# Fused attention and two feed-forward layers: adjacent heads as pairs, keys on 128 partitions, whole w_in transfers, TensorE turning the first q

## The chip, the cores and the metric

One core of one Trainium2 chip runs the kernel. The metric is the device time of one execution in microseconds. The kernel before was timed three times. Besides that there is a profiled execution, from which all rows below come.

## The reference

```python
# q, k, v: (8 batches, 8 heads, 576 tokens, 64); float32. w_in etc.: float64
k_p = k.reshape(B, H, 72, 8, D).mean(axis=3)          # keys and values pooled by 8
v_p = v.reshape(B, H, 72, 8, D).mean(axis=3)
scores = scale * np.matmul(q, k_p.transpose(0, 1, 3, 2))
attn = softmax(scores)                                 # exp(x - max) / (sum + 1e-9)
x = matmul(attn, v_p) -> (4608 tokens, 512)            # heads side by side
h = x @ w_in; g = h * np.cos(h); y = g @ w_out         # 512 -> 2048 -> 512
g = y @ w_gate; silu = g / (1 + exp(-g))               # 512 -> 1536
out = (silu * (y @ w_val)) @ w_out2                    # 1536 -> 512
```

The weights come as float64 and are converted on the chip, two 32-bit words to one number.

## The kernel before

The stages run on one another. Attention goes batch by batch (8 batches of 576 tokens) in tiles of 128 tokens, the fifth of 64 (`TILES`). The first feed-forward layer goes in 9 blocks of 512 tokens, each of 16 slots (one slot a block of 128 of the 2048 hidden rows): `pe_h` makes a hidden block, the scalar and vector engines its cosine, `pe_y` adds its part of the output, two slots later. The attention of batches 1 to 7 is spread over those slots by the tables MID, LATE, EXP and NORM with START. Batch 0 runs alone ahead of slot 0 by the string `program`: s is the scores of a tile (`do_s`, and then `do_qt` of the next tile), x its softmax, p the turning of the probabilities, a the product with the values, V and K and U the pooling sums, f a few steps of weight conversion, i and o loads of w_in and w_out, q the load of batch 1's q, X the split of the first block of x. The second layer follows from slot 128 on in products of a fast matrix scheme; the change doesn't touch it.

Heads are paired for TensorE: two heads of 64 dimensions lie on the 128 partitions. Before, head p and head p + 4 make pair p (`(r p)` in the views). `kT` holds a pair's keys in blocks, so that one matmul gives both heads' scores.

q: `load_q` (line 143) reads a batch in four transfers, one for each half r of the heads and each half e of the 64 dimensions, into 32 partitions each, in runs of 32 numbers (128 bytes); ACT_QUEUE says which batches' halves the scalar engine (ACT) issues instead of SyncE (SP). `do_qt` (line 257) turns a tile in blocks of 32x32 on VectorE (DVE).

Keys: the raw keys lie on 72 partitions, one for each pooled position, 8 tokens x 64 numbers in a row. `pool_sum` halves the row three times by additions (lines 190 and 192). Batch 0's raw keys come in two transfers into `kst`, batch 1's in four into buffers of w_in (`load_kv1`), both are summed on DVE. Later batches come in pieces by `do_raw`, one piece a slot, and are summed on GpSimd (POOL). `prep_k` turns the sums on TensorE and ACT scales them into `kT`.

Weights: `cv_load` (line 438) issues a unit's load. A unit of w_in is 128 rows of 512 numbers (4 KB a row), read as two halves of 64 rows to 64 partitions, because a pair's two heads stand 256 rows apart in w_in. A unit of w_out is 128 rows in one transfer. The conversion is a run of DVE instructions (lines 445, 456, 462, 467, 473) with one on ACT (451).

Order: the code is traced in Python, and the Tile layer's scheduler puts each engine's instructions in an order from its own estimate of times. On an engine that order is fixed. A transfer's issue waits on its queue for what it needs, and so does all behind it.

Of the kernel before, what the change touches and what calls it, by code (L numbers as in the profile page):

```python
# [8 lines left out]
F32 = mybir.dt.float32  # L9
# [16 lines left out]
def fused_kernel(  # L26
# [42 lines left out]
    ACT_QUEUE = {(0, 0), (3, 1), (1, 1), (3, 0), (1, 0)}  # L69
# [14 lines left out]
    xhl = const.tile([P, 2, KC, TB], F32R, name="xhl")  # L84
# [71 lines left out]
    pairs = "(r p) (s l) d -> r s p (l d)"  # L156
    kview = [k[b].rearrange(pairs, r=2, l=POOL) for b in range(B)]
    vview = [v[b, :, : SM * POOL].rearrange(pairs, r=2, l=POOL) for b in range(B)]
    vleft = [v[b, :, SM * POOL :].rearrange("h (s l) d -> h s (l d)", l=POOL) for b in range(B)]

    def load_kv(b, kind, i):

        rows = SP if kind == "k" else P
        t = kvraw[b, kind, i] = p1a.tile([P, POOL * D], F32, name=f"{kind}raw_{b}_{i}", tag="kv", bufs=2)[:rows]
        if kind == "k":
            nc.sync.dma_start(t, kview[b][i % 2, :, i // 2])
# [4 lines left out]
    def load_kv1():  # L171

        for p in range(NP):
            t = wts.tile([P, 2, TB], F32, name=f"k1_{p}", tag=f"wa3{p}")
            nc.sync.dma_start(t[:SP], kview[1][:, :, p].rearrange("r s x -> s r x"))
            kraw1.append(t[:SP])
# [20 lines left out]
    def new_kp(b):  # L197
        kps[b] = p1a.tile([SP, NP, 2, D], F32, name=f"kp_{b}", tag="kp")
# [4 lines left out]
    def sum_kv(b, kind, i):  # L203
        if i == 0:
            (new_kp if kind == "k" else new_vp)(b)
        dst = kps[b][:, i // 2, i % 2] if kind == "k" else vps[b][:, i]
        pool_sum(nc.gpsimd, dst, kvraw.pop((b, kind, i)))

    def prep_k(b):

        kp = kps.pop(b)
        ps = psum.tile([P, NP, SP], F32, name=f"kps_{b}", tag="att", bufs=2)
        for p in range(NP):
            nc.tensor.transpose(ps[:, p], kp[:, p].rearrange("s r d -> s (r d)"), ident[:SP, :SP])
        nc.scalar.mul(kT[0:64, :, 0:SP], ps[0:64], -EXP_SCALE)
        nc.scalar.mul(kT[64:128, :, SP:], ps[64:128], -EXP_SCALE)

    def prep_v(b):
        vmh, vml, vl1, vl2 = (av_tile(nm, b) for nm in ("vmh", "vml", "vl1", "vl2"))
        vp = vps.pop(b)  # L220
        if b < ACTB:
            for r in range(2):
# [5 lines left out]
                mask[:SM].rearrange("q (r p o) -> q r p o", r=2, o=1).to_broadcast([SM, 2, NP, D]),  # L228
# [13 lines left out]
        t = t.rearrange("q (r p) d -> q r p d", r=2)  # L242
# [48 lines left out]
    def do_norm(b, t, pm=None):  # L291
# [16 lines left out]
        for g in range(2):  # L308
            left = pm[:n, H * SM + g * SM : H * SM + (g + 1) * SM].rearrange("q (r p s) -> q p r s", r=2, p=NP)
            if g == 0:  # L310
                nc.vector.tensor_mul(
                    left,
                    e[:, :, SM:].rearrange("q (p r) s -> q p r s", r=2),
                    sm.rearrange("q (p r) o -> q p r o", r=2).to_broadcast([n, NP, 2, SL]),
                )
# [51 lines left out]
    raws = [(b, kind, i) for b in range(2, B) for kind, m in (("k", H), ("v", NP + 1)) for i in range(m)]  # L367

    def do_raw(b, i):
        at = (b - 2) * (H + NP + 1) + i  # L370
# [46 lines left out]
    for b in range(1, B):  # L417
# [3 lines left out]
        if b + 1 < B:  # L421
            for i in range(H + NP + 1):
# [9 lines left out]
    def cv_load(key, src, home=None):  # L432
        st = raw_tile(f"st_{key}") if home is None else wts.tile([P, 2, TB], F32, name=f"st_{key}", tag=home)
        st = st.rearrange("p a t -> p (a t)")
        src = src if isinstance(src, list) else [src]
        m = P // len(src)
        for i, x in enumerate(src):
            nc.sync.dma_start(st[i * m : (i + 1) * m].bitcast(U64), x)
# [46 lines left out]

    def x_split(half):
# [771 lines left out]
```

## Time and profile before

| | us |
|---|---|
| median of 3 timed runs | 1805.19 |
| lowest and highest | 1802.82, 1806.52 |
| the profiled execution | 1804.83 |
| its span | 1803.1 |
| busy: PE, DVE, ACT, POOL | 1737.5, 1263.8, 1066.6, 171.7 |

The span is the time from the core's first instruction to its last. Busy time is the time in which an engine has at least one instruction under way. PE is TensorE's matmuls, PEld its weight loads; SPq and ACTq are transfers' issues on those engines, whose data moves later. The 16 DMA engines are shared by all queues; q1 is SP's, q10 ACT's.

### The profile page before, as it was taken

The page shows a single profiled execution, that of the slowest core. Times are in us where ns is not written, and L with a number is a line of the kernel's source. Part 1 is how long each engine was busy: PE and PEld are TensorE (multiplying, and loading weights), DVE is VectorE, ACT ScalarE, POOL GpSimd, SP SyncE. Part 2 cuts the span into 40 slices and gives each one's busy share as a digit, 9 for nine tenths or more (in the row PEclk, how much of TensorE's full clock was granted, in tenths as well). Part 3 has the DMA queues.
Part 4 walks back from the last instruction along what each step waited for, and adds up shares of the span by engine and source line. Part 5 has one row for each costly group of instructions (what it writes and reads, how often), then busy time and mean ns, then how long its engine had stood idle before and what let it go on. Part 6 is the DMA issues. An engine that isn't in the chain of part 4 may idle for free.

```text
span 1803.1 us, 23421 instructions
## 1 busy us (share of the span) xinstructions
PE 1737.5 (96%) x8044; PEld 1439.4 (80%) x8044; DVE 1263.8 (70%) x2152; ACT 1066.6 (59%) x1933; POOL 171.7 (10%) x254
## 2 busy tenths in 40 slices
PE   2879999999999999999999999999999999999998
PEld 2546587888878888878877888888888888999998
DVE  6898688877877677787875586863584367358446
ACT  3578587777777767778776565533443344344333
POOL 0150513304104022000000000000000000000000
PEclk9989999999999999999999999999999999999999
DMA  9934246446566455474885488576667556787773
GB/s 186 203 104 120 79 165 188 156 131 197 148 205 218 114 198 144 158 220 153 235 275 176 159 320 291 193 252 225 194 200 267 193 192 221 290 265 246 294 249 93
DMA packets 248157, 357.01 MB, mean 198 GB/s; under 512 B 149608, under 2 KB 155752, under 8 KB 248040
## 3 DMA queue, kind: packets, MB, share of 16 engines
q1 hardware_dynamic: 224840, 352.58, 61.7%
q10 hardware_dynamic: 23200, 2.95, 1.1%
q8 instruction: 64, 1.05, 0.2%
q14 instruction: 53, 0.43, 0.1%
HBM read 285.74 MB, written 69.73 MB: 197 GB/s over the span
## 4 chain that ended last, share of the span: by engine, by line
PE 68%; DVE 14%; DMA 9%; ACT 5%; issue 2%; SPq 1%; POOL 0%; ACTq 0%; DVEq 0%
PE X L762 13%; PE oX L892 8%; PE Y L762 7%; PE h L507 4%; PE h L509 4%; PE h L508 4%; PE acc L578 4%; PE oY L892 4%; PE acc L579 4%; PE acc L577 4%; PE Z L762 3%; DMA w2r<-w_dram 2%; PE oZ L892 2%; PE av L358 2%; PE acc L570 2%
## 5 line engine op out<-in xcount | busy, mean ns | idle before, releaser
L762 PE MATMUL X<-t_P,wc 128*128 128x512 f32 (+1 forms) x1080 | 232.6, 367 | 1.0 <-ACT u L811 1.0
L507 PE MATMUL h<-xhl,wa 128*128 128x512 f32 x576 | 231.5, 402 | 0.0
L508 PE MATMUL h<-xhl,wa 128*128 128x512 f32 x576 | 226.3, 393 | 1.3 <-DVE xhl L131 1.3
L509 PE MATMUL h<-xhl,wa 128*128 128x512 f32 x576 | 225.6, 392 | 0.0
L762 PEld LDWEIGHTS X<-t_P,wc 128*128 128x128 f32 x1080 | 196.5, 188 | 27.5 <-ACT u L811 2.4
L578 PE MATMUL acc<-gl,wo_ring 128*128 128x512 f32 x448 | 176.4, 394 | 1.7 <-DVE gl L558 1.5
L577 PE MATMUL acc<-gh,wo_ring 128*128 128x512 f32 x448 | 175.1, 401 | 3.1 <-ACT gh L555 2.9
L579 PE MATMUL acc<-gh,wo_ring 128*128 128x512 f32 x448 | 175.4, 391 | 0.0
L544 DVE SCALAR_TENSOR_TENSOR w<-w,hs 128x512 f32<-128x512 f32 x144 | 102.3, 710 | 49.7 <-ACT w L541 48.4
L516 ACT ACTIVATE hs<-h 128x512 f32<-128x512 f32 x144 | 85.7, 595 | 76.4 <-DVE w L544 47.8
L540 ACT ACTIVATE w<-w 128x512 f32<-128x512 f32 x144 | 91.0, 632 | 64.9 <-DVE w L519 63.8
L507 PEld LDWEIGHTS h<-xhl,wa 128*128 128x128 f32 x576 | 108.7, 189 | 25.7 <-issue 4.1
L508 PEld LDWEIGHTS h<-xhl,wa 128*128 128x128 f32 x576 | 108.7, 189 | 25.3 <-issue 2.4
L509 PEld LDWEIGHTS h<-xhl,wa 128*128 128x128 f32 x576 | 108.5, 188 | 23.8 <-issue 0.9
L519 DVE SCALAR_TENSOR_TENSOR w<-w,hs 128x512 f32<-128x512 f32 x144 | 105.3, 731 | 23.7 <-ACT w L518 23.5
L814 DVE TENSOR_TENSOR p<-p,X 128x512 f32<-128x512 f32 (+1 forms) x60 | 37.9, 632 | 117.0 <-PE X L762 109.5
L558 DVE TENSOR_TENSOR gl<-w,gh 128x512 fp32r<-128x512 f32 x128 | 90.9, 710 | 40.2 <-ACT gh L555 38.6
L130 ACT CAST xhl<-pst 128x1024 fp32r<-128x1024 f32 (+1 forms) x70 | 67.7, 967 | 71.3 <-PE oX L892 26.1
L518 ACT ACTIVATE w<-hs,few 128x512 f32<-128x512 f32 x144 | 104.5, 725 | 7.3 <-DMA w_dram<-ce_w 4.2
L892 PE MATMUL oX<-xhl,wc 128*128 128x512 f32 (+1 forms) x480 | 102.8, 368 | 0.0
L578 PEld LDWEIGHTS acc<-gl,wo_ring 128*128 128x128 f32 x448 | 84.6, 189 | 21.5 <-DVE gl L558 5.2
L577 PEld LDWEIGHTS acc<-gh,wo_ring 128*128 128x128 f32 x448 | 84.1, 189 | 21.7 <-ACT gh L555 4.9
(197 smaller groups left out, 3586.3 us busy)
## 6 DMA issues: line engine op xcount, KB each, us to landing
wc<-wc_dram SPq DMA_DIRECT2D x273, 512.0 KB
wo_ring<-wo_dram SPq DMA_DIRECT2D x112, 512.0 KB
wc_dram<-wc SPq DMA_DIRECT2D x42, 512.0 KB
wc_dram<-ow SPq DMA_DIRECT2D x42, 256.0 KB
y_dram<-yo SPq DMA_DIRECT2D x18, 512.0 KB
w_dram<-ce_w SPq DMA_DIRECT2D x36, 256.0 KB
st_i<-in_moe_w_in_dram SPq DMA_DIRECT2D x32, 256.0 KB
st_o<-in_moe_w_out_dram SPq DMA_DIRECT2D x16, 512.0 KB
```

The lines of the kernel that those rows point to most:

```text
L507: nc.tensor.matmul(ps, whi, xhl[:, 0, c], start=c == 0, stop=False)
L508: nc.tensor.matmul(ps, whi, xhl[:, 1, c], start=False, stop=False)
L509: nc.tensor.matmul(ps, wlo, xhl[:, 0, c], start=False, stop=c == KC - 1)
L518: nc.scalar.activation(w, h, AF.Identity, bias=magic)
L519: nc.vector.scalar_tensor_tensor(out=w, in0=w, scalar=MAGIC, in1=h, op0=ALU.subtract, op1=ALU.subtract)
L540: nc.scalar.activation(w, w, AF.Sin, scale=PI)
L544: nc.vector.scalar_tensor_tensor(out=w, in0=w, scalar=1.0, in1=h, op0=ALU.subtract, op1=ALU.mult, reverse0=True)
L577: nc.tensor.matmul(acc[n][i], a[:, cols], xh, start=f == 0, stop=False)
L578: nc.tensor.matmul(acc[n][i], a[:, cols], xl, start=False, stop=False)
L579: nc.tensor.matmul(acc[n][i], b[:, cols], xh, start=False, stop=f == NF1 - 1)
L762: nc.tensor.matmul(ps[:, :hb], w, t[:, x, c, :hb], start=first and c == 0 and n == 0, stop=c == 1 and n == 2, skip_group_check=not first,)
L892: nc.tensor.matmul(banks[key][m][:, :hb], u, x[:, b, i, :hb], start=first_ and j == i == k == 0, stop=j == NJ - 1 and i == 1 and k == 2, s ...
```

## The change

Heads 2p and 2p + 1 become pair p, in the views of q, k and v and in the masks. With that the 128 rows of w_in for a pair lie together, and a unit is one transfer to 128 partitions.

The raw keys go on 128 partitions: 64 pooled positions of one pair above 64 of the next, four such pieces a batch (NP), and the last 8 positions of all pairs as two pieces of 32 partitions (`kleft`). A batch of keys is six pieces instead of eight, in ten transfers; batches 0 and 1 are read in six transfers each. The sums take three groups instead of four.

Batch 0's q no longer goes through `load_q`. It comes in five transfers on ACT's queue, one a tile, with tokens on partitions and runs of 64 numbers (256 bytes), into the space that `xhl` takes later. TensorE turns it, four transposes a tile into PSUM, and ACT copies it out. The other batches keep DVE's turning, but the heads of one half no longer make one constant step together with the tokens, so `load_q` issues each of the four parts pair by pair: 16 transfers of 72 KB, all on SP; ACT_QUEUE goes.

```diff
-    ACT_QUEUE = {(0, 0), (3, 1), (1, 1), (3, 0), (1, 0)}
...
-    qview = q.rearrange("b (r p) (t i) d -> b r i p t d", r=2, i=32)
+    qview = q.rearrange("b (p r) (t i) d -> b r i p t d", r=2, i=32)
...
-                (nc.scalar if (b, r) in ACT_QUEUE else nc.sync).dma_start(
-                    qi[a : a + 32].rearrange("i p (t d) -> i (p t) d", d=32),
-                    qview[b, r, :, :, :, 32 * e : 32 * e + 32].rearrange("i p t d -> i (p t) d"),
-                )
+                for p in range(NP):
+                    nc.sync.dma_start(
+                        qi[a : a + 32, p].rearrange("i (t d) -> i t d", d=32), qview[b, r, :, p, :, 32 * e : 32 * e + 32]
+                    )
+    q0 = const.tile([P, 2, KC, TB], F32, name="q0", tag="xhl").rearrange("p a c t -> p (a c) t")
+
+    def load_q0():
+        for t, (t0, n) in enumerate(TILES):
+            nc.scalar.dma_start(
+                q0[:n, t].rearrange("s (h d) -> s h d", h=H), q[0, :, t0 : t0 + n].rearrange("h s d -> s h d")
+            )
...
+    NK = NP + 2
+    kview = [k[b, :, : SM * POOL].rearrange("(g x r) (s l) d -> g x s r (l d)", x=2, r=2, l=POOL) for b in range(B)]
+    kleft = [k[b, :, SM * POOL :].rearrange("(p r) (s l) d -> r s p (l d)", r=2, l=POOL) for b in range(B)]
...
-        for p in range(NP):
-            nc.tensor.transpose(ps[:, p], kp[:, p].rearrange("s r d -> s (r d)"), ident[:SP, :SP])
-        nc.scalar.mul(kT[0:64, :, 0:SP], ps[0:64], -EXP_SCALE)
-        nc.scalar.mul(kT[64:128, :, SP:], ps[64:128], -EXP_SCALE)
+        for g in range(2):
+            nc.tensor.transpose(ps[:, g * P : (g + 1) * P], kp[:, 2 * g : 2 * g + 2].rearrange("s r d -> s (r d)"), ident)
+        m = SL * NP
+        nc.tensor.transpose(ps[:, 2 * P :], kp[:m, NP:].rearrange("s r d -> s (r d)"), ident[:m, :m])
+        for r in range(2):
+            rows = slice(r * D, (r + 1) * D)
+            to = kT[rows, :, r * SP : (r + 1) * SP]
+            nc.scalar.mul(to[:, :, :SM], ps[rows, : 2 * P].rearrange("d (p s) -> d p s", p=NP), -EXP_SCALE)
+            nc.scalar.mul(to[:, :, SM:], ps[rows, 2 * P :].rearrange("d (s p) -> d p s", p=NP), -EXP_SCALE)
...
+        if b == 0:
+            ps = psum.tile([P, NP, n], F32, name=f"qp_{t}", tag="hg", bufs=2)
+            for p in range(NP):
+                nc.tensor.transpose(ps[:, p], q0[:n, t, p * P : (p + 1) * P], ident[:n, :n])
+            nc.scalar.copy(qT, ps)
+            return
...
-                src = [w_in[(r * NP + c) * D : (r * NP + c + 1) * D, j * TB : (j + 1) * TB] for r in range(2)]
-                cv_load(keys[u], src, f"wa{j}{c}")
+                cv_load(keys[u], w_in[c * P : (c + 1) * P, j * TB : (j + 1) * TB], f"wa{j}{c}")
...
-    for r in range(2):
-        nc.sync.dma_start(kst4[:, r], kview[0][r])
+    for g in range(2):
+        for x in range(2):
+            nc.sync.dma_start(kst[x * SM : (x + 1) * SM, 2 * g : 2 * g + 2], kview[0][g, x])
+    for r in range(2):
+        nc.sync.dma_start(kst[: SL * NP, NP + r], kleft[0][r])
...
-    load_q(0)
+    load_q0()
...
-    for r in range(2):
-        pool_sum(nc.vector, kps[0][:, :, r], kst4[:, r])
+    for g in range(2):
+        pool_sum(nc.vector, kps[0][:, 2 * g : 2 * g + 2], kst[:, 2 * g : 2 * g + 2])
+    pool_sum(nc.vector, kps[0][: SL * NP, NP:], kst[: SL * NP, NP:NK])
...
-        "K0 K1 K2 K3 U0 x4 k b i3 f6 "
+        "K0 K1 K2 U0 x4 k b i3 f6 "
```

## Rows read from the trace of the kernel before

**Rows 1.** The page's busy times: us, share of the span, instructions.
```profile
PE 1737.5 (96%) x8044; PEld 1439.4 (80%) x8044; DVE 1263.8 (70%) x2152; ACT 1066.6 (59%) x1933; POOL 171.7 (10%) x254
```
**Rows 2.** Busy time by stretch: us, engines' busy us, granted clock, DMA share, GB/s.
```profile
0.00:72.45 72.45, 36.21 (x93) 20.71 (x93) 48.73 (x103) 30.57 (x105) 5.97 (x21) 1.00 0.96 196
72.45:139.15 66.70, 55.49 (x199) 35.05 (x199) 66.24 (x112) 48.63 (x128) 31.84 (x41) 0.92 0.47 125
139.15:1803.10 1663.95, 1645.81 (x7753) 1383.63 (x7753) 1148.88 (x1938) 987.37 (x1701) 133.90 (x192) 1.00 0.62 201
```
**Rows 3.** The chain that ended last: start us, us, what.
```profile
47.95 9.49 DMA qi<-in_q_dram
...
63.74 8.69 DMA st_i<-in_moe_w_in_dram
...
139.15 1.12 PE acc L570 x2
```
**Rows 4.** Busy time by stretch, columns as in the second group: halves alone, whole loads.
```profile
48.00:51.00 3.00, 3.00 (x6) 1.18 (x5) 3.00 (x9) 0.53 (x2) 0.00 (x0) 1.00 1.04 246
...
63.00:65.00 2.00, 2.00 (x5) 0.86 (x4) 1.44 (x4) 0.37 (x1) 0.00 (x0) 1.00 1.03 400
```
**Rows 5.** DVE's groups to 72.5 us: shapes, count, busy us, mean ns, idle before.
```profile
L445 DVE TENSOR_SCALAR ce_i<-st_i 128x512 uint32<-128x512 uint32 x8 | 3.3, 420 | 7.1 <-DMA st_i<-in_moe_w_in_dram 7.1
...
L257 DVE STREAM_TRANSPOSE qT<-qi 128x512 f32<-128x512 f32 x4 | 2.8, 703 | 0.0
...
L190 DVE TENSOR_TENSOR k<-k 72x512 f32<-72x512 f32 x4 | 2.6, 671 | 0.0
...
L190 DVE TENSOR_TENSOR k<-k 72x256 f32<-72x256 f32 x4 | 1.6, 416 | 0.0
...
L445 DVE TENSOR_SCALAR wo<-st_i 128x512 uint32<-128x512 uint32 x1 | 0.4, 427 | 0.4 <-DMA st_i<-in_moe_w_in_dram 0.4
```
**Rows 6.** The DMA view of 371 to 380 us, batch 4's q.
```profile
DMA packets 9434, 1.75 MB, mean 194 GB/s; under 512 B 9295, under 2 KB 9295, under 8 KB 9434
```
**Rows 7.** PE in time: start us, us, line, operation, count, idle before and releaser.
```profile
18.17 0.71 PE L214 MATMUL kps<-ident,kp 72*128 72x72 f32 x4 [18.17 <-DVE kp L192]
24.66 2.26 PE L269 MATMUL s<-kT,qT 128*128 128x144 f32 x8 [5.78 <-DVE qT L257]
...
35.77 1.12 PE L326 MATMUL pt<-ident,pm 128*128 128x128 f32 x4 [1.01 <-ACT kst L279]
...
58.86 0.42 PE L330 MATMUL px<-ident,kst 128*64 128x128 f32 x1 [3.17 <-ACT ring L364]
```
**Rows 8.** ACT in time, columns as in the group before.
```profile
36.93 0.58 ACT L328 COPY pth<-pt 128x512 f32<-128x512 f32 x1
...
57.83 0.72 ACT L451 ACTIVATE ce_i<-ce_i,few 128x512 int32<-128x512 int32 x1 [4.55 <-DMA qi<-in_q_dram]
...
282.59 0.60 ACT L516 ACTIVATE hs<-h 128x512 f32<-128x512 f32 x1 [3.78 <-DMA qi<-in_q_dram]
```
**Rows 9.** SP's issues in time: start us, us with waits between, line, count.
```profile
41.47 9.06 SPq L438 DMA_DIRECT2D st_i<-in_moe_w_in_dram  x8
60.52 0.84 SPq L438 DMA_DIRECT2D st_o<-in_moe_w_out_dram  x2
...
162.27 4.40 SPq L148 DMA_DIRECT2D qi<-in_q_dram  x3
```
**Rows 10.** SP's own waits: who for whom, us in total, times, longest us.
```profile
SPq L438 <- DMA qi<-in_q_dram: 16.9, 2, 10.0
```
**Rows 11.** DMA queues, 66 to 76 us: packets, MB, share of 16 engines.
```profile
q1 hardware_dynamic: 703, 2.31, 93.2%
q10 hardware_dynamic: 1053, 0.13, 10.7%
```
**Rows 12.** DMA queues, 51 to 56 us, columns as before.
```profile
q10 hardware_dynamic: 2246, 0.29, 52.8%
q1 hardware_dynamic: 183, 0.57, 47.7%
```

More of the change, by code (lines that the diff above doesn't have):

```diff
@@ L171, in load_kv1 @@
     def load_kv1():
-        for p in range(NP):
-            t = wts.tile([P, 2, TB], F32, name=f"k1_{p}", tag=f"wa3{p}")
-            nc.sync.dma_start(t[:SP], kview[1][:, :, p].rearrange("r s x -> s r x"))
-            kraw1.append(t[:SP])
+        for g in range(3):
+            t = wts.tile([P, 2, TB], F32, name=f"k1_{g}", tag=f"wa3{g}")
+            kraw1.append(t if g < 2 else t[: SL * NP])
+            if g < 2:
+                for x in range(2):
+                    nc.sync.dma_start(t[x * SM : (x + 1) * SM], kview[1][g, x])
+            else:
+                for r in range(2):
+                    nc.sync.dma_start(t[: SL * NP, r], kleft[1][r])
         for j in range(0, NP + 1, 2):
@@ L197, in new_kp @@
     def new_kp(b):
-        kps[b] = p1a.tile([SP, NP, 2, D], F32, name=f"kp_{b}", tag="kp")
+        kps[b] = p1a.tile([P, NK, D], F32, name=f"kp_{b}", tag="kp")
     def new_vp(b):
@@ L211, in prep_k @@
         kp = kps.pop(b)
-        ps = psum.tile([P, NP, SP], F32, name=f"kps_{b}", tag="att", bufs=2)
-        for p in range(NP):
-            nc.tensor.transpose(ps[:, p], kp[:, p].rearrange("s r d -> s (r d)"), ident[:SP, :SP])
-        nc.scalar.mul(kT[0:64, :, 0:SP], ps[0:64], -EXP_SCALE)
-        nc.scalar.mul(kT[64:128, :, SP:], ps[64:128], -EXP_SCALE)
+        ps = psum.tile([P, NP * SP], F32, name=f"kps_{b}", tag="att", bufs=2)
+        for g in range(2):
[7 more added lines that the diff above has]
+            nc.scalar.mul(to[:, :, SM:], ps[rows, 2 * P :].rearrange("d (s p) -> d p s", p=NP), -EXP_SCALE)
     def prep_v(b):
@@ L365, in do_av @@
             done += m
-    raws = [(b, kind, i) for b in range(2, B) for kind, m in (("k", H), ("v", NP + 1)) for i in range(m)]
+    raws = [(b, kind, i) for b in range(2, B) for kind, m in (("k", NK), ("v", NP + 1)) for i in range(m)]
     def do_raw(b, i):
-        at = (b - 2) * (H + NP + 1) + i
+        at = (b - 2) * (NK + NP + 1) + i
         if at + 1 < len(raws):
@@ L421, in fused_kernel @@
         if b + 1 < B:
-            for i in range(H + NP + 1):
+            for i in range(NK + NP + 1):
                 at(lates, START[b] + i + (b == 1), do_raw, b + 1, i)
@@ L434, in cv_load @@
         st = st.rearrange("p a t -> p (a t)")
[L435 to L438, printed above, removed]
+        nc.sync.dma_start(st.bitcast(U64), src)
         cv[key] = st.rearrange("p (t two) -> p t two", two=2)
@@ L483, in chain_tile @@
         return chain.tile([P, TB], dtype, name=nm, tag=tag, bufs=bufs)
+    xhl = []
     def x_split(half):
+        if not xhl:
+            xhl.append(const.tile([P, 2, KC, TB], F32R, name="xhl", tag="xhl"))
         for c in range(KC):
             src = ring[:, c, half * TB : (half + 1) * TB]
-            split(xhl[:, 0, c], xhl[:, 1, c], src)
+            split(xhl[0][:, 0, c], xhl[0][:, 1, c], src)
     wa = {}
@@ L831, in out_steps @@
         own = pools2["a"].tile([P, 2, 2, TB], F32R, name=f"op_{q}", tag="tP7")
-        homes = [own, xhl[:, :, 0:2], xhl[:, :, 2:4]]
+        homes = [own, xhl[0][:, :, 0:2], xhl[0][:, :, 2:4]]
         b11, b12, b21, b22 = ((e, h) for e in range(2) for h in range(2))
@@ L1006, in fused_kernel @@
     vst = p1w.tile([P, 8, TB], F32, name="vst", tag="big1", bufs=1)
-    kst4 = kst[:SP].rearrange("s (p r) x -> s r p x", r=2)
     load_i(1)
+    for g in range(2):
+        for x in range(2):
+            nc.sync.dma_start(kst[x * SM : (x + 1) * SM, 2 * g : 2 * g + 2], kview[0][g, x])
     for r in range(2):
-        nc.sync.dma_start(kst4[:, r], kview[0][r])
+        nc.sync.dma_start(kst[: SL * NP, NP + r], kleft[0][r])
     load_i(1)
     fill(2)
-    load_q(0)
+    load_q0()
     load_i(1)
```

37 lines of the change are left out of this document (16 added, 21 removed).

## The prediction

> **What bounds the kernel now.** I read the busy times first, then three stretches of the span, then the chain that ended last, and only then the queues. TensorE (PE) is busy 96% of the span [rows 1], but not evenly. From 139.15 us to the end it is busy 1645.8 of 1664 us, so that stretch is TensorE's own work. Before it lie two others: to 72.45 us PE is busy half the time, VectorE (DVE) two thirds, and the DMA engines 96%; from 72.45 to 139.15 us DVE is busy 66.24 of 66.70 us [rows 2]. The chain says the same: transfers carry it up to 72.4 us, DVE up to 139.1, PE after that [rows 3]. None of TensorE's matmuls after 139 us changes in count or shape, apart from the keys' transposes (three a batch for four), so what the change is worth is how much earlier the point at 72.45 us comes. DVE then works through the same 66 us, and PE through the same 1664 us. A microsecond won there is one at the end, as long as PE's own start moves with it.
>
> **The sum's base.** The profiled execution took 1804.83 us with a span of 1803.1; the median of the three timed runs is 1805.19, 0.36 above it. I make the sum against 1804.83 and add 0.36. A measurement of this kernel can tell about 0.2%, 3.6 us, from no change.
>
> **w_in in whole units.** Now a unit of w_in (128 rows of 4 KB) goes in two halves to 64 partitions each. While nothing but halves was moving, the DMA engines were full at 246 GB/s; while mostly whole 128-partition loads (w_out's) were moving they were just as full at 400 GB/s [rows 4]. The change makes w_in's units such loads. Ten units count up to 72.45 us: DVE has begun on eight and then on one [rows 5], and the tenth is the one that the chain waits for until 72.4 [rows 3]. Ten of 0.524 MB take 21.3 us at 246 GB/s and 13.1 at 400. That is 8.2 us less of a resource that is full; the bounds are 0 (other traffic sharing the engines sets the rate) and 8.2, and I take the upper one, because the engines are 96% busy and the two rates come from neighbouring stretches.
>
> **q of batch 0 in token rows.** It was 1.18 MB in 128-byte pieces, half issued by SP, half by ScalarE's queue (ACT). A later batch of the same loads moved at 194 GB/s with the engines full [rows 6], so it costs 6.1 us. Pieces of 256 bytes on 128 partitions are not in the trace. The nearest rows are these 194 and the 400 of [rows 4], so the new cost is between 6.1 and 2.9 us, the gain between 0 and 3.2; I take the middle, 1.6. DMA path together: 9.8 us.
>
> **Keys on 128 partitions.** The bytes are the same; two transfers become six (kst), four become six (batch 1), eight a batch become ten later on. Half-tiles of 64 rows stay half-tiles, so I cost the transfer at nothing, bounds one microsecond either way. On DVE the additions of a batch take 3 groups instead of 4 of 512, 256 and 128 columns: of the 2.6 + 1.6 us of the two larger additions [rows 5] a quarter goes, 1.05, and with the smallest some 1.3 us for batch 1; batch 0 has the same columns in other groups, between 0 and 1.3. The DVE transposes of q go as well, four of 0.70 us [rows 5] and one of half the width, 3.2 us. Together some 5 us of DVE's 48.7 before 72.45 us. It is not added to the DMA term: the two run side by side, and DVE is idle for 23.7 us there [rows 2], mostly for data. GpSimd's sums of later batches get shorter, off the path.
>
> **TensorE turning q.** Each 128-token tile adds four transposes and one ACT copy out of PSUM. The same shapes stand in the trace: four transposes of 128x128 take 1.12 us [rows 7], and the copy of pt out of PSUM 0.58 [rows 8]. Five tiles are 5 us of PE and 3 of ACT in a stretch where PE idles 36 us [rows 2]; the DVE transpose that they replace also stood between two score steps. So I cost them at nothing, with 2 us as the upper bound if ACT's exponentials stand ahead of the copy. In exchange the first scores no longer need all of q. They start at 24.66, 5.78 us after PE's last key transpose, for want of q [rows 7]; with one tile of q they can follow the keys. That, and SP no longer placing q between the keys and the next weights, I value at 6 us (5 to 8).
>
> **ACT without q.** Batch 1's q is issued on ACT, and ACT then stands for 4.55 us, its next instruction waiting for q [rows 8]; the chain runs through that transfer, 9.49 us [rows 3]. PE stands 3.17 us because ACT's ring copy is behind it [rows 7]. In the changed kernel these issues are SP's: 3.2 us for PE's chain. Attention's chain from first scores to the first hidden matmul thus gains 6 + 3.2 = 9.2 us, the DMA chain 9.8. The later one counts: **9 us**.
>
> **What SP takes over.** Every later q is now 16 transfers of 72 KB on SP instead of four of 288 KB. What stands behind them in SP's order: for batch 1 the first w_out loads, a key load and w_in's later units, for batch 2 the w_out loads, later the w_out ring. For batch 1 SP today issues w_in until 50.5 us and then stands 10.0 us for a q transfer before it issues w_out at 60.52 [rows 9, 10]. With the DMA some 8 us ahead, SP comes to q at about 42, and has until 60.5 before it is late against today: 1.16 us an issue. The trace has no issue of a quarter's size. A free issue of one DMA is about 0.4 us (w_out's two take 0.84), three big ones in a row took 4.40, 1.47 each [rows 9]. I take 0.5, near the first, because a quarter of the packets fills a queue a quarter as much: 8 us, free from 50 us on.
>
> Here the skill speaks against the change. The Trainium skill, "SBUF — State Buffer", section "The DMA setup-cost knee", says that each transfer pays about 2 us whatever its size, and measures 64 KiB transfers at 138 GB/s. If the 16 paid that one after the other, an estimate from that page is 32 us, w_out at 74 instead of 60.5, and the time 1818. The trace doesn't bear that out: three issues in 4.40 us [rows 9] overlap.
>
> **Later batches.** Behind 139 us PE hides what SP does, as far as these rows show; bounds 4 us either way. One thing may come back: ACT stands 3.78 us for batch 3's q at 282.6 us [rows 8], and that wait goes.
>
> **Forecast**: 1804.83 - 9 + 0.36 = **1796 us**, its own range 1791 to 1801, chance 48%.
>
> **Rivals.**
> *Q's tiles arrive late* (22%). ACT's queue shares the 16 DMA engines with SP's. How much it gets differs by an order: beside a steady stream of SP's w_in packets 1053 of its packets went with 703 of SP's, 1.5 to one [rows 11]; earlier 2246 with 183, 12 to one [rows 12]. At 12 the tiles are there long before their scores. At 1.5 the 3072 packets of tiles 1 to 3 need 2050 packets of SP's, some 5.5 MB at 2.7 KB each, about 27 us at 200 GB/s. Issued at about 8 us they land at 35 to 39, where the fourth scores would want theirs by 33. Attention loses 6 of its 9 us: 1802, range 1800 to 1804. For it speaks that SP is now never held up by q. The rule beside it, from "DMA: Bandwidth & Descriptors" in the Trainium skill, section "Queues, rings and completion order", is that each engine goes round its queues packet by packet; by that, the ratio of rows 11 is the one for a full SP queue.
>
> *More than the sum* (16%). If DVE fills the idle time that the earlier transfers open (it has 23.7 us there, and 5 us less to do), the point moves by 14 rather than 9, and batch 3's lost ACT wait gives 3: 1788, range 1784 to 1791.
>
> *Whole units no faster* (8%). If the mixed traffic, not the halves, holds the rate at 246, only DVE's 5 us are left: 1800.
>
> *SP held up* (6%), the slower one. If a small issue costs 1.47 us like the big ones, 16 take 23.5 us, w_out's load comes at 42 + 23.5 = 65.5 instead of 60.5, and DVE's conversion behind it 5 us later: 1810. It decides above 1.16 us an issue. Against it speaks only that a quarter of the packets stands behind each issue.
>
> **Chances.** Faster by over 0.2% (below 1801.6): nearly all of the forecast, the 16%, most of the 8% and some two fifths of the 22%, 0.79. Within 0.2%: the rest of the 22% and a third of the slower case, 0.15. Slower (above 1808.8): 0.06. The range from 1787 to 1804 leaves out the far half of the 16%, the slower case and a tail of late tiles, under 2 in 10.
>
> **What would show it.** Right: w_in's loads one issue each, near 400 GB/s where they run alone; first scores at 17 to 20 us; no ACT wait for q near 57 us; the first hidden matmul 8 to 10 us earlier than now; PE's solid stretch from about 130. Wrong: score matmuls waiting for q's ACT copies (late tiles), or SP's q issues near 1.5 us each with DVE waiting for w_out or w_in behind them. New PE gaps after 139 us would say that moving q to SP is not free there, and the forecast would fail without any step up to 72 us being wrong.

## The result, and the profile after

The changed kernel takes 1818.1 us (median; 1814.6 to 1822.8) against 1805.2 for the kernel before. The ratio is 1.0071, with a 95% interval of 1.0049 to 1.0093: 0.7% slower, clear of noise, where 1796 had been forecast and 1804 was the upper end. The profiled execution took 1818.1 us with a span of 1816.4.

The same three stretches as in [rows 2], and the last of them in two parts, up to 250 us and behind (us, busy us of PE, PEld, DVE, ACT and POOL, granted clock, DMA share, GB/s), of the changed kernel:

```profile
0.00:72.45 72.45, 48.93 (x143) 30.39 (x143) 42.68 (x99) 35.67 (x130) 6.01 (x22) 1.00 0.87 209
72.45:139.15 66.70, 50.96 (x161) 30.85 (x162) 56.18 (x102) 42.02 (x99) 20.49 (x24) 0.85 0.30 98
139.15:1816.40 1677.25, 1654.20 (x7755) 1385.09 (x7753) 1147.98 (x1948) 992.75 (x1726) 118.64 (x173) 0.99 0.61 200
...
139.15:250.00 110.85, 100.61 (x327) 58.60 (x326) 79.35 (x143) 70.46 (x154) 34.36 (x45) 0.91 0.38 110
250.00:1816.40 1566.40, 1553.59 (x7430) 1326.49 (x7428) 1068.63 (x1805) 922.29 (x1572) 84.28 (x128) 1.00 0.63 206
```

and these two parts of the kernel before:

```profile
139.15:250.00 110.85, 107.42 (x402) 68.86 (x403) 87.53 (x161) 78.31 (x160) 30.77 (x40) 1.00 0.39 116
250.00:1803.10 1553.10, 1538.39 (x7353) 1314.77 (x7351) 1061.35 (x1778) 909.06 (x1542) 103.13 (x152) 1.00 0.64 207
```

Up to 72.45 us the change does what was forecast: TensorE has been busy 48.93 us, not 36.21 [rows 2]. After that the picture turns. DVE, which was full in the second stretch (66.24 of 66.70), is now idle for more than 10 us of it; TensorE is busy 4.5 us less, and its clock is granted at 0.85 instead of 0.92. The loss arises before 250 us: from 72.45 us to there TensorE idles 26.0 us, where it idled 14.6 before. Behind 250 us it idles 12.8 us, before 14.7, so nothing more is lost there, and the loss is not made good.

The start, in PE's instructions in time (start us, us, line, operation, count, idle before and what ended it), of the changed kernel:

```profile
18.96 2.29 PE L297 MATMUL s<-kT,qT 128*128 128x144 f32 x8 [1.69 <-ACT kT L238]
...
64.56 0.80 PE L532 MATMUL h<-xhl,wa 128*128 128x512 f32 x1
```

and the first hidden matmul of the kernel before:

```profile
71.54 0.80 PE L507 MATMUL h<-xhl,wa 128*128 128x512 f32 x1
```

The first scores come at 18.96 us, not 24.66 [rows 7], and the first hidden matmul 7.0 us earlier.

Now DVE in time between 82 and 102 us, in the changed kernel:

```profile
82.38 0.69 DVE L544 SCALAR_TENSOR_TENSOR w<-w,hs 128x512 f32<-128x512 f32 x1 [0.23 <-ACT w L543]
...
84.43 0.69 DVE L569 SCALAR_TENSOR_TENSOR w<-w,hs 128x512 f32<-128x512 f32 x1 [0.76 <-ACT w L566]
86.53 0.69 DVE L544 SCALAR_TENSOR_TENSOR w<-w,hs 128x512 f32<-128x512 f32 x1 [1.42 <-ACT w L543]
...
92.81 0.69 DVE L569 SCALAR_TENSOR_TENSOR w<-w,hs 128x512 f32<-128x512 f32 x1 [1.36 <-ACT w L566]
...
94.05 0.39 DVE L466 TENSOR_SCALAR wo<-st_o 128x512 uint32<-128x512 uint32 x1
...
101.03 0.65 DVE L494 SCALAR_TENSOR_TENSOR wo<-st_o,wo 128x512 f32<-128x512 f32 x1
```

and the same first and last step of the first unit's conversion in the kernel before:

```profile
64.66 0.43 DVE L445 TENSOR_SCALAR wo<-st_o 128x512 uint32<-128x512 uint32 x1 [0.53 <-DMA st_o<-in_moe_w_out_dram]
...
85.24 0.67 DVE L473 SCALAR_TENSOR_TENSOR wo<-st_o,wo 128x512 f32<-128x512 f32 x1
```

The lines L544 and L569 are DVE's two steps of a slot's cosine. In the changed kernel those of the first four slots stand ahead of w_out's first conversion, which therefore starts at 94.05 us instead of 64.66. The unit is ready some 16 us later (101.03 against 85.24), since before its steps lay further apart. DVE waits for ACT between them, although w_out can be converted: SP issued it at 55.38 us (below), and by 80 us its DMA engines have nothing left to move. The slice from 80 to 90 us, in the columns of the stretches above:

```profile
80.00:90.00 10.00, 8.29 (x24) 6.26 (x24) 5.51 (x9) 7.23 (x14) 0.00 (x0) 0.66 0.00 0
```

SP's issues in time, of the changed kernel:

```profile
38.07 17.27 SPq L147 DMA_DIRECT2D qi<-in_q_dram  x16
55.38 0.97 SPq L459 DMA_DIRECT2D st_o<-in_moe_w_out_dram  x2
...
166.66 1.95 SPq L147 DMA_DIRECT2D qi<-in_q_dram  x4
172.20 0.35 SPq L459 DMA_DIRECT2D st_o<-in_moe_w_out_dram  x1
172.59 6.77 SPq L147 DMA_DIRECT2D qi<-in_q_dram  x12
...
211.73 9.01 SPq L175 DMA_DIRECT2D kraw<-in_k_dram  x2
223.84 2.06 SPq L181 DMA_DIRECT2D vraw<-in_v_dram  x3
226.00 0.54 SPq L459 DMA_DIRECT2D st_o<-in_moe_w_out_dram  x1
```

What this does to TensorE is in its waits from 72.45 to 250 us (who for whom, us in total, times, longest us). In the changed kernel:

```profile
PE acc L595 <- DVE wo L494: 13.7, 6, 6.8
PE h L532 <- ACT hs L541: 7.1, 5, 2.7
```

and in the kernel before:

```profile
PE acc L570 <- DVE w L544: 9.2, 4, 4.4
PE acc L570 <- DVE wo L473: 3.4, 3, 2.4
```

The wait for w_out's converted units has grown from 3.4 to 13.7 us. The longest, 6.8 us, is near 230 us: there the last w_out unit stands on SP behind key and value pieces (226.00 above). So there were two candidates from the start: the order of instructions, and SP's queue.

### The profile page after: what moved, and what is told of

It reads as the page before. It is cut to its first block, busy times and chain, and to the rows that moved or that the text cites. A ratio compares the mean times of both kernels' runs of the same rounds, so it can differ in the third digit from the quotient of the medians.

```text
span 1816.4 us, 23555 instructions
## 1 busy us (share of the span) xinstructions
PE 1754.1 (97%) x8056; PEld 1446.3 (80%) x8056; DVE 1246.8 (69%) x2147; ACT 1070.4 (59%) x1952; POOL 145.1 (8%) x218
## 4 chain that ended last, share of the span: by engine, by line
PE 77%; DVE 11%; DMA 6%; ACT 4%; issue 1%; POOL 1%; SPq 0%; DVEq 0%; ACTq 0%; POOLq 0%
PE X L787 14%; PE oX L917 8%; PE Y L787 7%; PE h L532 5%; PE h L533 5%; PE h L534 5%; PE acc L603 5%; PE acc L602 5%; PE acc L604 5%; PE oY L917 4%; PE Z L787 4%; PE av L382 3%; PE s L297 2%; PE oZ L917 2%; PE acc L595 2%
## 5 line engine op out<-in xcount | busy, mean ns | idle before, releaser
L569 DVE SCALAR_TENSOR_TENSOR w<-w,hs 128x512 f32<-128x512 f32 x144 | 102.2, 710 | 55.8 <-ACT w L566 54.6
L544 DVE SCALAR_TENSOR_TENSOR w<-w,hs 128x512 f32<-128x512 f32 x144 | 104.5, 725 | 23.6 <-ACT w L543 23.3
```

Of the source, the lines that this page charges most:

```text
L544: nc.vector.scalar_tensor_tensor(out=w, in0=w, scalar=MAGIC, in1=h, op0=ALU.subtract, op1=ALU.subtract)
L569: nc.vector.scalar_tensor_tensor(out=w, in0=w, scalar=1.0, in1=h, op0=ALU.subtract, op1=ALU.mult, reverse0=True)
```

## The experiments

Each kernel was timed beside the kernel before on the same chip. **Theory A** was that moving batch 1's q to SP makes the build put w_out's conversion behind four slots of cosine. **Rival B** was that sixteen small transfers are slow in themselves. **Rival C** was that w_out stands on SP behind key and value pieces.

### Which queue, how many transfers

```diff
# q_act: the changed kernel
-                    nc.sync.dma_start(
+                    (nc.scalar if b in (1, 3) else nc.sync).dma_start(
# before_4sp: the kernel before
-    ACT_QUEUE = {(0, 0), (3, 1), (1, 1), (3, 0), (1, 0)}
+    ACT_QUEUE = {(0, 0)}
# before_16 (all on SP but the first half of batch 0's) and before_16act (queues kept): the kernel before
-                (nc.scalar if (b, r) in ACT_QUEUE else nc.sync).dma_start(
...
+                for p in range(NP):
...
# four_q, four_q_sp: the changed kernel with the old load_q and its view, ACT_QUEUE kept or empty
```

**q_act.** 

> The changed kernel with one thing put back: the 16 q transfers of batches 1 and 3 are issued by ACT's queue, as their four were before; batch 2's stay on SP. All else as changed. Theory A (with batch 1's q on SP, the order of DVE's instructions, fixed when the program is built, puts w_out's first conversion and batch 1's qT behind four attention slots' cosine work; DVE then stands idle from 80 to 98 us and runs behind until 160): the first w_out conversion comes at 75 to 85 us instead of 94, DVE is busy over 9 us in 80:90, and the time is 1793 to 1803. Rival B (sixteen small transfers are slow wherever they are issued): ACT now stands about 17 us for its issues, the ring copies behind it are late, and the time stays at 1810 to 1820.

Measured: 1810.3 us, ratio 1.0027 (1.0016 to 1.0038). The time is just inside rival B's range, and part of B shows: ACT issues q up to 73.7 us, its other work stands 5.31 us until 74.1, and DVE waits 5.53 us for q up to 81.94. The conversion of w_out begins at 68.02 us, earlier even than A had it, but its fifth unit is now late, and DVE waits for that:

```profile
120.07 0.43 DVE L466 TENSOR_SCALAR wo<-st_o 128x512 uint32<-128x512 uint32 x1 [3.99 <-DMA st_o<-in_moe_w_out_dram]
```

**four_q.** 

> The changed kernel with the later batches' q in four transfers again, batches 1 and 3 on ACT's queue as before the change. (These four read q for heads p and p+4 where the changed kernel reads 2p and 2p+1, so the scores of batches 1 to 3 use other heads' q; sizes and counts of everything else stay.) Theory A: as with the sixteen on ACT, 1793 to 1803, perhaps 2 us less since ACT issues less. Rival B (number and size of the transfers is the cost): also 1793 to 1803; this run tells A from B only together with the next.

Measured: 1821.1 us, 1.0085 (1.0068 to 1.0102). This was another mechanism. ACT's queue issues batch 1's q already at 13.43 and 18.96 us, the second scores wait 11.62 us for ACT's copy of their q, and the first hidden matmul comes only at 87.37 us. It looks like the prediction's rival of late tiles, but the tile was there: TensorE had turned it by 13.7 us. The copy, at 33.61 us, stands in ACT's order behind a conversion step that waits 9.66 us for DVE, and behind the first softmax.

```profile
29.98 0.72 ACT L473 ACTIVATE ce_i<-ce_i,few 128x512 int32<-128x512 int32 x1 [9.66 <-DVE ce_i L467]
```

```profile
34.29 2.29 PE L298 MATMUL s<-kT,qT 128*128 128x144 f32 x8 [11.62 <-ACT qT L284]
```

It says nothing on A or B.

**four_q_sp.** 

> As the kernel with four transfers a batch, but all of them on SP and none on ACT. (The scores of batches 1 to 3 again use other heads' q.) Theory A (the queue, not the number, sets DVE's order): DVE's idle time at 80 to 98 us is back although SP needs only some 6 us for q, and the time is 1812 to 1820. Rival B (the sixteen issues hold up SP): SP is free ten microseconds earlier, DVE is fed, and the time is 1793 to 1803.

Measured: 1813.1 us, 1.0046 (1.0029 to 1.0063), as A had it: w_out's first conversion comes at 93.67 us, behind the cosines of four slots. The number of transfers is worth some 4 to 5 of the changed kernel's 13 us, and the two intervals overlap.

**before_16.** 

> The kernel before, with one thing of the change alone: every q transfer but the first half of batch 0's is on SP, in quarters (16 a batch). Theory A: DVE's order is lost here too, w_out's first conversion comes behind slot 3's cosine work, and the time is 1812 to 1825 (none of the change's gains is in it). Rival B: slower by the time that SP loses, also over 1808. Rival C (the loss comes from the keys on 128 partitions or from q by TensorE, not from q's queue): no change, 1802 to 1808.

Measured: 1826.0 us, 1.0117 (1.0102 to 1.0132), a microsecond above A's range, with w_out's first conversion at 104.63 us, behind the cosines of four slots; B asked only for more than 1808. Rival C of this expectation is another than the C above; it falls, since neither the keys nor batch 0's q were changed here.

**before_4sp.** 

> The kernel before with one thing alone: batch 1's and batch 3's q, still four transfers of 288 KB a batch, are issued by SP instead of half by ACT. Theory A (the queue changes the fixed order): 1815 to 1828, as with sixteen on SP (1826). Rival B (the number and size of the transfers): within 4 us of the kernel before, 1801 to 1809.

Measured: 1823.8 us, 1.0101 (1.0086 to 1.0116), as A had it. The edit moves all four transfers of batch 1 and all four of batch 3, not half of them. SP is at w_out at 58.49 us, 2 us earlier than in [rows 9], so a late issue of w_out is not what costs the 20 us.

**before_16act.** 

> The kernel before with the later q in quarters (16 transfers a batch) on the queues that it had, ACT's for batches 1 and 3 and the same halves for batch 0. Theory A: DVE's order keeps w_out's conversion ahead of the cosines, and the time is 1801 to 1810. Rival B (number and size): 1815 to 1828, near the 1826 of sixteen on SP.

Measured: 1823.7 us, 1.0101 (1.0082 to 1.0119), as B had it. So the queue alone costs 20 us, the number alone costs 20, and both together 22. They are not two causes that add up; they look like two ways of upsetting one thing. What the three kernels have in common is that the build has ordered the instructions anew. How it came out differs: in before_4sp w_out's first conversion comes at 104.03 us, behind the cosines of four slots, as in the changed kernel; in before_16act it comes at 80.85, ahead of slot 0's cosine (93.77), and DVE waits 13 us for loads instead. That second shape was not taken apart further.

### Two attempts at a single cause

```diff
# hold: the changed kernel; conv_last holds the DVE instructions that fill() traced
+    def held(i):
+        return tc.issue_after(conv_last[-1]) if 0 <= i < 16 else nullcontext()
...
-        turns(s)
+        with held(i):
+            turns(s)
...
-        cosine(s)
+        with held(i):
+            cosine(s)
# act_gp: q_act with the pieces of batches 2 to 7 on POOL's queue, in load_kv (three places)
-                nc.sync.dma_start(
+                (nc.sync if b < 2 else nc.gpsimd).dma_start(
```

**hold.** 

> The changed kernel with every transfer where the change puts it (16 q transfers on SP), and one constraint on the order alone: in block 0 the cosine's DVE operations of a slot are queued behind the last weight conversion that the program traces before them. No wait is added between engines. Theory A (DVE's order is the cause): the first w_out conversion comes before slot 0's cosine, DVE is busy over 8 us in each of 80:90 and 90:100, and the time is 1796 to 1808. Rival B (SP's 17 us of q issues): nothing changes, 1812 to 1820. Rival C (the w_out loads stand on SP behind key and value pieces that wait for POOL, whatever DVE's order): a part comes back, 1806 to 1813, with PE gaps of several microseconds at wo left.

Measured: 1819.2 us, 1.0073 (1.0055 to 1.0091). The time is in the range in which B had nothing changed, but DVE's order did change: w_out's first conversion comes at 82.61 us, ahead of slot 0's cosine, and DVE is busy 8.74 and 10.00 us of the two 10 us slices. Theory A falls in this form: with the conversions ahead of the cosines, other instructions come too late. TensorE waits 14.1 us for the cosine and 8.5 for q's turning; the wait for w_out is down to 5.3.

**act_gp.** 

> The kernel with q of batches 1 and 3 on ACT (1810), and the key and value pieces of batches 2 to 7 issued by POOL instead of SP, so that no w_out load stands behind a piece that waits for a POOL sum. Rival C (that wait makes the gaps of 7.96 us at 118 and 3.46 at 222): they go, with the half clock behind them, and the time is 1795 to 1804. If C is wrong, or POOL loses as much by issuing, 1807 to 1815.

Measured: 1810.3 us, 1.0029 (1.0014 to 1.0043), as q_act. The gap of 7.96 us became one of 4.67, the wait for w_out's units fell from 5.0 to 2.7 us, and the time stayed. So clearing SP does not bring the time back; whether C is wrong or POOL lost as much by issuing, this run does not tell.

### The order itself, written out

**Theory O** takes the place of A: the loss is the whole order that came out differently, not the place of one instruction. To test it I wrote the order of the kernel before into other kernels. The lists name the instructions that both kernels have; the edges constrain the order on an engine and add no wait between engines.

```diff
+ORDER = [
+    [
+        555, 628, 550, 554, 562, 565, 614, 637, 433, 435, 534, 564, 699, 563, 437, 445, 613, 455, 439, 581,
...
+    traced = {i.name: i for i in nc.cur_bb.bb.instructions}
+    for line in ORDER:
+        for a, b in zip(line, line[1:]):
+            tc.add_manual_dep(
+                traced[f"I-{b}"], f"I-{a}",
+                mybir.DependencyInfo(mybir.DependencyClass.NoSync, mybir.DependencyReason.DATA), reason="order",
+            )
```

**order_all** (275 instructions of DVE, 427 of PE, 206 of ACT, 49 of SP). 

> The changed kernel, every transfer and operation as in it (q in 16 transfers on SP), with the order of the kernel before written out: from slot 0 to slot 20 the instructions that both kernels have stand on DVE, PE, ACT and SP in the order in which they stand before the change (constraints of order alone, no waits). Theory O (the fixed order that came out differently is the loss, wherever q is issued): the start's gain stays and the rest runs as before, 1790 to 1801; PE idle from the first hidden matmul to 160 us falls from 19 to about 11 us, and the time at half clock from 31 to about 10. Rival S (SP's longer q issues, or small transfers): the waits move to the loads and the time stays over 1808.

Measured: 1805.1 us, 1.0000 (0.9990 to 1.0011): 13 us of the loss are gone, but the range of Theory O (to 1801) was missed.

**order_dve** (the 275 of DVE alone). 

> As the kernel with the order of before on four engines, but on DVE alone. Theory O with DVE as the engine that decides: within 4 us of the kernel with all four, 1790 to 1803. If the orders of SP, ACT and PE matter as well: 1803 to 1815.

Measured: 1803.9 us, 1.0001 (0.9991 to 1.0011), as with all four engines: DVE's order alone brings as much back. The time is 1 us above the range for that.

**before16_order.** 

> The kernel before with q of the later batches in 16 transfers on SP (1826 with the order that the build chose), and with the order of the kernel before written out on DVE, PE, ACT and SP from slot 0 to slot 20. Theory O: 1801 to 1811, back near the kernel before. Rival S: 1815 to 1828.

Measured: 1812.7 us, 1.0047 (1.0032 to 1.0062), 2 us above O's range.

**before_neworder.** 

> The kernel before, no transfer changed, with the order of the changed kernel written out on DVE, PE, ACT and SP from slot 0 to slot 20. Theory O: the loss without the change, 1815 to 1830. Rival S: 1801 to 1809.

Measured: 1830.1 us, 1.0142 (1.0127 to 1.0157). This is the plainest of them: no transfer and no operation of the kernel before is changed, only the order is that of the changed kernel, and 26 us are lost. DVE is busy 46.77 us of the second stretch, where it was full before:

```profile
72.45:139.15 66.70, 52.13 (x181) 33.27 (x179) 46.77 (x88) 41.53 (x107) 13.28 (x16) 0.90 0.34 91
```

In the other direction 13 to 14 us come back. But the start's gain was still missing: the changed kernel with the old order was only as fast as the kernel before. DVE in time, of order_dve:

```profile
48.64 0.42 DVE L486 TENSOR_SCALAR ce_i<-st_i 128x512 uint32<-128x512 uint32 x1
63.14 0.69 DVE L497 SCALAR_TENSOR_TENSOR ce_i<-st_i,ce_i 128x512 uint32<-128x512 uint32 x1 [14.09 <-ACT ce_i L492]
```

and ACT, whose step L492 it waits for:

```profile
59.82 0.37 ACT L408 COPY ring<-av 128x256 f32<-128x256 f32 x1 [1.28 <-PE av L402]
...
62.12 0.37 ACT L408 COPY ring<-av 128x256 f32<-128x256 f32 x1 [1.28 <-PE av L402]
62.39 0.72 ACT L492 ACTIVATE ce_i<-ce_i,few 128x512 int32<-128x512 int32 x1
```

ACT's step is ready at 49 us and stands behind ring copies, each of which waits for TensorE's attention. So DVE stands 14.09 us ahead of slot 0, before the lists begin. In before16_order the same wait is 12.7 us.

### The order from 48 us on, and the parts with it

The lists now begin where w_in's fifth unit is converted, with 287 instructions of DVE and 237 of ACT.

**after2.** 

> The changed kernel, nothing but order constrained: DVE and ACT take the order of the kernel before from the first conversion step of w_in's fifth unit (at about 48 us) on, not only from slot 0 on. With the shorter constraint (1804) DVE stood 14.1 us at 49 to 63 us because ACT's step of that conversion came behind ring copies that wait for TensorE. Theory O2 (this fixed order on ACT held back the gain): DVE works through that stretch, waits at most 5 us for w_out, PE's 8 us wait at 65 goes, and the time is 1792 to 1800. Rival S (SP's 17 us of q issues make w_out late and take the same time): DVE then waits for w_out's load instead, 1801 to 1806.

Measured: 1796.5 us, 0.9947 (0.9927 to 0.9966). The same program as the changed kernel in another order, 21.6 us faster, and at the forecast of the prediction; that it lands there is in part luck, as the terms below show. Its stretches:

```profile
0.00:72.45 72.45, 48.44 (x140) 29.40 (x141) 52.05 (x114) 36.43 (x132) 7.08 (x23) 1.00 0.93 232
72.45:139.15 66.70, 56.23 (x194) 34.07 (x193) 64.29 (x113) 51.67 (x124) 28.29 (x34) 0.90 0.30 93
139.15:250.00 110.85, 108.53 (x425) 72.96 (x424) 85.68 (x161) 80.97 (x162) 25.31 (x34) 1.00 0.40 119
```

Against the changed kernel's, DVE has done 9.4 us more by 72.45 us. From there to 250 us TensorE is busy 164.76 us, not 151.57: 13.2 us less idle. The rows know two levels of the clock, 1.00 and 0.50, so a stretch with a mean clock c stands 2(1 - c) of its time at half: 20 and 20 us in the changed kernel, 13 and 0 in this one, 27 us less, which is worth at most 13. The two make 26.5 at most; the spans differ by 21.6. Some of the half clock lies in idle time.

**before16_order2.** 

> The kernel before with q of the later batches in 16 transfers on SP, DVE and ACT in the order of the kernel before from the same point on. With the shorter constraint it took 1812.7. Theory O2: the 13.6 us for which DVE stood for ACT go, SP issues w_out some 4 us later than before, and the time is 1802 to 1809. Rival S: 1810 to 1815.

Measured: 1807.9 us, 1.0027 (1.0016 to 1.0038). With the order kept, SP's 16 transfers cost the kernel before 3.8 us by the medians, 4.9 by the ratio. SP comes to w_out 6 us later than in [rows 9]:

```profile
53.27 13.25 SPq L184 DMA_DIRECT2D qi<-in_q_dram  x16
66.56 0.97 SPq L473 DMA_DIRECT2D st_o<-in_moe_w_out_dram  x2
```

**act2.** 

> As the first of this call, with q of batches 1 and 3 issued by ACT again, 16 transfers each. Theory O2: SP is free for w_out ten microseconds earlier, so 1790 to 1799, if ACT's issues do not hold back its other work; if they do (rival), 1800 to 1810, with DVE or PE waiting for ACT between 45 and 70 us.

Measured: 1802.5 us, 0.9994 (0.9980 to 1.0008), with runs from 1797 to 1808; the rival's range. In the profiled execution, the fastest of them, DVE waits 6.1 us for ACT, once, up to 68.5 us. So the sixteen issues on ACT cost 6 to 8 us against after2 even with the order kept.

**half2.** 

> As the first of this call, but each unit of w_in again as two transfers of 64 rows. If the term for w_in's units (8.2 us of full DMA) counts at the end: 4 to 9 us slower than the first. If the transfers are hidden behind the order and the other engines: within 2 us of it.

Measured: 1797.6 us, 0.9965 (0.9952 to 0.9977): 1.2 us slower than after2 by the medians, 3 by the ratios, and the intervals overlap. The whole units are worth little at the end. A reason can be read in SP's issues of after2 (whole units):

```profile
38.27 16.68 SPq L182 DMA_DIRECT2D qi<-in_q_dram  x16
54.99 0.97 SPq L494 DMA_DIRECT2D st_o<-in_moe_w_out_dram  x2
```

and of half2:

```profile
42.84 12.15 SPq L182 DMA_DIRECT2D qi<-in_q_dram  x16
55.04 2.13 SPq L497 DMA_DIRECT2D st_o<-in_moe_w_out_dram  x2
```

With halves SP is 4.6 us later at q, gets through q 4.5 us sooner, and is at w_out at the same moment.

**oldq2** (batch 0's q through `load_q(0)` and DVE again). 

> As the changed kernel with DVE and ACT in the order of the kernel before from 48 us on (1796.5), but batch 0's q goes the old way: blocks of 32x32 turned by DVE, no transposes on TensorE, in 16 transfers, half on ACT's and half on SP's queue. If the gain is the attention chain (scores that no longer wait for all of q): 5 to 9 us slower, 1801 to 1806, with the first scores at 23 to 27 us. If the gain comes from DVE and the transfers instead: within 2 us, 1794 to 1799.

Measured: 1799.6 us, 0.9975 (0.9964 to 0.9986), 3.1 us slower than after2 by the medians, 5 by the ratios; the intervals just touch, and the time lies between the two expected ranges. The first scores are at 22.25 us:

```profile
22.25 2.26 PE L319 MATMUL s<-kT,qT 128*128 128x144 f32 x8 [5.99 <-DVE qT L307]
```

**mid2**, the step order of `program`: `i1 o2 q` in place of `i1 q o2`. 

> As the changed kernel with DVE and ACT in the order of the kernel before from 48 us on (1796.5), with one step moved: the program loads w_out's first two units before batch 1's q, so SP issues them some 17 us earlier. In the kernel that this is compared with DVE stands 3.21 and 1.03 us for these loads at 55 to 60 us. If that wait counts at the end (SP's q issues cost 4 us, as before16_order2 against the kernel before says): 1790 to 1794. If it is hidden: 1795 to 1798.

Measured: 1794.0 us, 0.9946 (0.9929 to 0.9962). It has the lowest median here, but the ratio is that of after2, so the run does not decide between its two expectations. SP issues w_out at 39.11 us, and DVE's wait moves on to w_in:

```profile
64.67 0.43 DVE L501 TENSOR_SCALAR wo<-st_i 128x512 uint32<-128x512 uint32 x1 [5.36 <-DMA st_i<-in_moe_w_in_dram]
```

| with the order kept from 48 us on | us | against the kernel before |
|---|---|---|
| kernel before, q in 16 on SP (before16_order2) | 1807.9 | 1.0027 |
| all of the change (after2) | 1796.5 | 0.9947 |
| ... w_in in halves (half2) | 1797.6 | 0.9965 |
| ... batch 0's q the old way (oldq2) | 1799.6 | 0.9975 |
| ... w_out ahead of q on SP (mid2) | 1794.0 | 0.9946 |

Against before16_order2, which has SP's q too, the rest of the change is worth 11.4 us; half2 and oldq2 account for some 4 of them (by the ratios, 8 of 14). The other 6 or 7, the keys' layout among them, were not taken apart.

## Why the prediction was wrong

**The step that failed** is at the end of the first part: "DVE then works through the same 66 us, and PE through the same 1664 us. A microsecond won there is one at the end". I read the second stretch as work of fixed length. It was full because of the order in which DVE's instructions stood, and that order is no property of the code: the build makes it, anew for each program. I had written in front of the prediction that the scheduler orders by its own estimate of times, and did not draw the conclusion that a change of a queue changes that order. The runs put numbers to it: the order alone costs the kernel before 26 us (before_neworder), and the changed kernel 21.6 (after2). Why the estimate tips over when q changes its queue or its size was not tested. That it does is shown by before_4sp, where nothing but the queue of eight transfers (batches 1 and 3) is changed and w_out's first conversion goes from 64.66 to 104.03 us; and for the sixteen transfers by before_16 and before16_order2, where the old order gives back 18 of 22 us.

That after2 comes out at 1796.5 does not confirm the sum of 9 us: its terms came out otherwise, as follows, and 6 or 7 us of what was won have no term that was measured.

**The start.** Right: first scores at 18.96 (17 to 20 forecast), no wait of ACT for q near 57 us. The first hidden matmul came 7.0 us earlier, not 8 to 10.

**w_in in whole units, 8.2 us.** The rate was right: between 70.6 and 72 us, where little but w_in moves, the slices of the changed kernel show 346 to 473 GB/s, 419 in the mean. The term was not: half2 puts it at 1 to 3 us at the end. I had chosen the upper bound because the engines were 96% busy; but SP's order sets when w_out is issued, and behind w_in stands q, which in these two traces takes up what w_in saves.

**q of batch 0 by TensorE.** The attention chain's 9.2 us, of which 6 for the first scores, came out as 3.1 to 5 when only this was taken back. TensorE's first hidden matmul was 3.5 us later there (65.61 against 62.10); DVE was busy 64.31 and 64.29 us of the 66.70 behind it.

**ACT without q.** The wait went, and something came that I had not looked for: ACT's order changed with it, ring copies went ahead of a conversion step. DVE stood 14.09 us for that step in order_dve; in the changed kernel itself it stood 8.14 us up to 56.7, for ACT's split of x behind the same ring copies. The first half of a step that is taken off an engine is the wait; the second is the order of what is left.

**SP's issues, 0.5 us each.** They took 1.08 us each at 38 us (17.27 for 16) and 0.55 at 167 us (1.95 and 6.77), where SP had issued only one w_out load shortly before each group, not four w_in units and the values. Half of the sixteen took 0.50 us or less even at 38 us, in after2; a few stood up to 3.9 us:

```profile
L182 SPq DMA_DIRECT2D qi<-in_q_dram x16: 311/496/3945, 38.3 to 54.5; - x16
```

So the price of most issues was right, and the long ones were left out. The trace puts 3.8 us of them down to waits for earlier value loads; what the rest stood for it does not say. The mean is twice the forecast and still under the 1.16 us from which the slower rival was to decide, and w_out was issued at 55.38, not after 60.52 [rows 9]. So the rival that ended on the right side had the wrong mechanism. "Free from 50 us on" is nearly right with the order kept: 3.8 to 5 us in the kernel before, and between nothing (by the ratios) and 2.4 us (by the medians) in the changed one (mid2).

**The estimate of 32 us.** The Trainium skill, "SBUF — State Buffer", section "The DMA setup-cost knee", led to an estimate of 32 us for the 16 transfers, and of 1818 us. That number was hit, and not by its reason: the 16 took 17.27 us, and by 80 us the DMA engines had nothing left to move, while DVE's order kept it from w_out until 94.

**Later batches behind 139 us.** "Behind 139 us PE hides what SP does" failed too: at 226.00 us w_out's last unit stands behind pieces that wait for POOL, and TensorE stands 6.8 us. With the order kept TensorE idles 2.3 us in that stretch (108.53 of 110.85).

**The late tiles' 27 us.** The 2.7 KB a packet in that rival stands in none of its rows: rows 11 give 3.3 and rows 12 give 3.1, which makes some 34 us. In the changed kernel the scores of batch 0 stand 0.73 us at most for ACT's copy of q.

**The chances.** Slower had 6%, all on one mechanism. New gaps after 139 us were named as what would refute the forecast, and they came.

## What to carry to other kernels

Where a build chooses the order of instructions, an edit has two effects, its own and that of the new order, and the second can be larger than all you have worked out: 26 us against 9 here. Before you judge an edit, compare the order on the engine that is full before and after, above all where the edit moves a transfer to another queue or splits it; then write the old order out and time the edit with it. An engine that is busy 99% of a stretch owes that to its order too, and the new order that an edit brings along may not keep it, as here.

## What the runs showed of the hardware

**TensorE's clock had a part in the loss**, at most 13 of the 26.5 us between the changed kernel and after2. In the changed kernel TensorE stood 6.84 us at 228 us. The granted clock was 0.50 between 234 and 240 us, and the next eight matmuls took 6.55 us, against 3.70 at full clock:

```profile
175.19 3.70 PE L595 MATMUL acc<-w,wo 128*128 128x512 f32 x8
...
234.90 6.55 PE L595 MATMUL acc<-w,wo 128*128 128x512 f32 x8 [6.84 <-DVE wo L494]
```

So this wait cost 6.84 us and then 2.85 more. The clock also fell without such a stop. In hold, TensorE was busy 10.00 and 9.21 us of the 10 us slices before and around the fall (granted clock 1.00, then 0.72); it did transposes of 64x64 and the product with the values, and had stood 0.64 and 0.15 us.

```profile
170.00:180.00 10.00, 10.00 (x38) 6.28 (x37) 4.67 (x10) 3.67 (x17) 0.00 (x0) 1.00 0.88 236
180.00:190.00 10.00, 9.21 (x26) 4.18 (x24) 0.00 (x0) 2.41 (x10) 0.59 (x2) 0.72 0.20 60
```

What tips it there, the runs don't show.

**At the start the clock column does not tell the clock.** It reads 1.00 up to the first change in a trace. In the changed kernel the same matmul takes 0.63 us and then 0.40 while the column shows 1.00 for both:

```profile
66.01 0.63 PE L532 MATMUL h<-xhl,wa 128*128 128x512 f32 x1
...
66.98 0.40 PE L532 MATMUL h<-xhl,wa 128*128 128x512 f32 x1
```

In act2, where the column shows 0.50 from 43.3 to 67.2 us, this matmul takes 0.63 there. So by the durations TensorE ran at half clock up to some 66.5 us in the changed kernel, and up to 78.5 us in the kernel before, and the 1.00 of the first stretch [rows 2] is not to be trusted in either. The 0.92 of the kernel before's second stretch would then be some 0.88, an estimate from these 6 us.

**The time of SP's issues depends on what stands before them, not on their number alone.** Sixteen transfers of 72 KB took 17.27 us on SP at 38 us and 8.72 at 167; four of 288 KB at the first place took 13.33 (four_q_sp):

```profile
37.62 13.33 SPq L147 DMA_DIRECT2D qi<-in_q_dram  x4
```

Four times the bytes in each, and the four take 4 us less than the sixteen, not a quarter of their time. With the order kept, the same sixteen took 16.68 us in after2, and 12.15 in half2, which comes to them 4.6 us later.
